# First quad's transposes in 64x64 tiles, and narrower idle matmuls around its first scores

## The chip, the cores and the metric

The kernel runs on one core of one Trainium2 chip. A core has five engines that run side by side: TensorE (PE in the profile, with its weight loads as PEld), VectorE (DVE), ScalarE (ACT), GpSimd (POOL) and SyncE (SP, which here only issues transfers). Sixteen DMA engines carry data between HBM and the core's memory, SBUF. TensorE writes its results to PSUM, which has eight banks, numbered 0 to 7. The metric is the device time of one execution, in microseconds (us); the median of several is compared.

## What is computed

A sigmoid attention over 8 batches of 12 heads (448 tokens, 64 numbers a head) is followed by a token mixer whose mixing matrix is made from its own input. All inputs and outputs are float32.

```python
def _attn_ref(q, k, v):
    S = q.shape[2]
    scale = 1.0 / np.sqrt(q.shape[-1])
    scores = scale * np.matmul(q, k.transpose(0, 1, 3, 2)) - np.log(S)
    attn = 1.0 / (1.0 + np.exp(-scores))
    return np.matmul(attn, v).astype(np.float32)

def _moe_ref(x, w_q, w_k, w_out):
    wq = x @ w_q
    wk = x @ w_k
    scale = 1.0 / np.sqrt(d_hyper)
    W_tok = scale * np.einsum('bsd,btd->bst', wq, wk)
    mixed = np.einsum('bst,btd->bsd', W_tok, x)
    return (np.maximum(mixed, 0.0) @ w_out).astype(np.float32)
```

The attention's output, with its heads side by side, is `x` of the second part.

## The kernel before

The work is cut into 24 quads, each with four heads of one batch (`quads`, numbered n). For a quad, q, k and v come in as float32 tiles of 448 KB (192 KB and 256 KB for the two pieces of the first quad's k), are cast to bfloat16 and, for q and k, transposed, so that the 64 numbers of a head lie along the partitions. A quad has seven score steps and seven value steps. One score step (`scores`) is four matmuls in 64x64 tiles of the array, 448 columns each, into a pair of PSUM banks, and one sigmoid on ScalarE over the pair (128x896), which writes bfloat16. One value step (`values`) is four such matmuls that add the sigmoid's output times v into a further pair of banks. The mixer's steps of the batches are threaded in between.

All engines' instructions are issued in the order in which the code stands; a hand-written string, `PLAN`, sets it, one letter per step. `S` is a score step, `P` or `p` a value step, `q` and `k` the transposes of a later quad's q and k by TensorE, `r` and `z` transposes by VectorE, `1` a cast on VectorE, `a` and `b` the transposes of the second quad's q and k. `F` is a matmul of zeros by zeros, 128x512, into a bank of its own (`spare`): nothing reads it. Which PSUM banks a step takes is listed in the same order in `BANKS`.

The loads are issued by SyncE in the order of the string `ORDER`, eight tiles in flight at most; a further load waits until the cast that reads its buffer's last tile has run. POOL does most of the casts (L192, L209, L215), from quad 2 on.

The start stands ahead of the plan. TensorE runs 32 matmuls of zeros (L690) while the first loads are under way. Then come the first quad's pieces: q is cast in two parts, tokens `IA` (four of seven blocks) on VectorE and `IB` (three) on ScalarE; k in two, `KA` (three) on VectorE and, later, `KB` (four), also on VectorE. `tr_part` transposes a part on TensorE and copies it out of PSUM into `qk[0]` (L804): `transposes_whole` uses the whole 128x128 array for each block of tokens, so that the two head halves of a block come out next to each other; `transposes`, which later quads use (line 229), takes four 64x64 tiles per block, and writes the two halves into two banks. `q` parts `IA` and `IB` and `k` part `KA` go before the plan's first letter; part `KB` is the letter `K`. The plan begins `FFSSSFFKSSF1S1ab`. A score step needs all of `qk[0]`'s q, and the block of k that it multiplies with: its first three need `KA` alone.

Of the kernel before, what the change touches and what calls it, by code (L numbers as in the profile page):

```python
# [17 lines left out]
def kernel(  # L18
# [12 lines left out]
    nc = tc.nc  # L31
# [4 lines left out]
    P = 128  # L36
    NI, NP = 7, 64
# [4 lines left out]
    HALF = (slice(0, 64), slice(64, 128))  # L42
# [21 lines left out]
    banks = ps_q.tile([P, 8, 512], F32, tag="banks", name="banks")  # L64
# [19 lines left out]
    def take(*ids):  # L84
        for b in ids:
            readers[b] = (readers[b][0] + readers[b][1], [])

    def bank2():
        lo, hi = (int(b) for b in BANKS.pop())
        take(lo, hi)  # L90
        assert hi == lo + 1
        return (lo, hi), banks[:, lo : hi + 1], banks16[:, lo : hi + 1]

    def bank1():
        b = int(BANKS.pop())
        take(b)
        return (b,), banks[:, b], banks16[:, b]

    def read(fb, inst, keep=False):

        for b in fb:
            for old in readers[b][0]:
                if not keep and old.ins.engine != inst.ins.engine:
                    tc.declare_no_dep(inst.ins, old.ins, reason="both only read the bank")
            readers[b][1].append(inst)
# [6 lines left out]
    zeros = singles.tile([P, 512], BF16)  # L112
# [12 lines left out]
    def xt(u, j):  # L125
# [4 lines left out]


    PLAN = (
        "FFSSSFFKSSF1S1abSSSSSPrPsPSPSzPqSkSSP1PSPSxPSrPSSPSPsPPPPPPP"
        "SPPSSzWWWSWWWSxSSrXSNPsPPPPSPSPUSzSPPPSRMSPPPSqkSSXMSSMSRPPC"
        "SP1xSPPPcSSWWWxSWdWSWSQSrNsSSOOOSPPPSPPSPzPISISISISPPPPPSPSc"
        "PodoSSxUSPPMSPRPSPPScWQWSdMSWWoWWSMPPSPPrPSPPSNQosSSzSQOQxSO"
# [84 lines left out]
    qk = {}  # L221
    ps_qk = {}

    def transposes(ps, t16, r):

        for x, i in enumerate(range(r.start, r.stop)):
            for g in range(2):
                for h in range(2):
                    nc.tensor.transpose(
                        ps[HALF[g], h, x * NP : (x + 1) * NP], t16[HALF[h], i, g, :],  # L230
                        ident16[HALF[h], HALF[h]],
                    )

    def transposes_whole(ps, t16, r):

        for x, i in enumerate(range(r.start, r.stop)):
            nc.tensor.transpose(
                ps[:, x * P : (x + 1) * P], t16[:, i].rearrange("p b d -> p (b d)"), ident16,
            )
# [75 lines left out]
    def scores(n, i):  # L315
        fb, sc, _ = bank2()
        for g in range(2):
            for h in range(2):
                nc.tensor.matmul(  # L319
                    sc[HALF[h], g, 0:S], qk[n][HALF[g], h, 1, i, :],  # L320
                    qk[n][HALF[g], h, 0].rearrange("p i n -> p (i n)"), start=True, stop=True,
                )
        at = at_bufs[len(sigmoids) % len(at_bufs)]
        inst = nc.scalar.activation(at, sc[:, :, 0:S], ACTF.Sigmoid, bias=attn_bias, scale=attn_scale)  # L324
        read(fb, inst)
        if len(sigmoids) >= len(at_bufs):

            tc.declare_no_dep(inst.ins, sigmoids[-len(at_bufs)].ins, reason="TensorE read the buffer in between")
        sigmoids.append(inst)
        ats[n, i] = at  # L330
# [3 lines left out]
    def values(n, i, tail, eng):  # L334
        u, j = quads[n]
        if i == 0:
            pv[n] = bank2()
        fb, ps, _ = pv[n]
        for h in range(2):
            for g in range(2):  # L340
                nc.tensor.matmul(  # L341
                    ps[HALF[g], h, 0:S], ld["v16", n][HALF[h], g, i, :],
                    ats[n, i][HALF[h], g, :], start=(i == 0), stop=(i == NI - 1),
                )
        if i == NI - 1:
            if tail:
                for h in range(2):
                    read(fb, COPY["vs"[h]](out=xt(u, j)[:, h, 0:S], in_=ps[:, h, 0:S]))
            else:
                read(fb, COPY[eng](out=xt(u, j)[:, :, 0:S], in_=ps[:, :, 0:S]))  # L350
# [323 lines left out]
    def cols(r):  # L674
# [9 lines left out]
        out=ident, in_=ident, compare_op=ALU.not_equal, fill=1.0, base=0,  # L684
# [1 line left out]
    )  # L686
    nc.vector.tensor_copy(out=ident16, in_=ident)
    nc.scalar.activation(warm, zeros[:, 0:1], ACTF.Sigmoid, bias=attn_bias, scale=1.0)
    for _ in range(32):
        nc.tensor.matmul(banks[:, 6, 0:P], zeros[:, 0:P], zeros[:, 0:P], start=True, stop=True)  # L690
    for t in xts:
        nc.vector.memset(t[:, :, S:], 0.0)
    for t in wqks:
# [76 lines left out]
    def pump():  # L770
        while pumped[0] < len(ORDER):
            nm, n = ORDER[pumped[0]]
            if (nm, n) not in OTHERS:
                if not ready(nm, n):
                    break
                cast_now(nm, n, "d" if (nm, n) in CASTING else "g")
            pumped[0] += 1

    def cast_next(e):
        nm, n = BY[e].pop(0)  # L780
        assert ready(nm, n) and (e == "v" or nm in "vw" or KIND[n] in "qa")
        cast_now(nm, n, e)
        pump()
# [16 lines left out]

    def tr_part(nm, t16, r, e):
        fb, _, ps = bank2()
        transposes_whole(ps[:, 0], t16, r)
        read(fb, COPY[e](  # L804
            out=qk[0][:, :, "qk".index(nm), r].rearrange("p h i n -> p i h n"),
            in_=ps[:, 0, 0 : (r.stop - r.start) * P].rearrange("p (i h n) -> p i h n", h=2, n=NP),
        ))

    tr_part("q", q016, IA, "v")
    tr_part("q", q016, IB, "s")  # L810
    tr_part("k", k016, KA, "v")
    cast_part(k016, k0, KB, "v")
    used |= {("q", 0), ("k", 0)}
# [6 lines left out]
    for t in PLAN:  # L820
        if t == "F":
            nc.tensor.matmul(bank1()[1], zeros[:, 0:P], zeros, start=True, stop=True)
            continue
        if t in "12":
            cast_next("vs"[int(t) - 1])
            continue
        kind = ALIKE.get(t, t if t in "qkx" else t.upper())
        c = done[kind]
        done[kind] += 1
        tail = done["S"] == N * NI  # L830
        if t == "S":
            scores(*divmod(c, NI))
        elif kind == "P":
            n, i = divmod(c, NI)
            values(n, i, tail or t == "R", "s" if t == "p" else "v")
            if i == NI - 1:
                used.add(("v", n))
                pump()
        elif kind in "qk":
            if t in "rs":  # L840
                quads_r.append(c) if t == "r" else None
                if t == "s":
                    quadrants(c, 0)
            tr(c, kind, t)
            if t in "df":
                used.add(("q", c))
            if t not in "cers":
                used.add((kind, c))
                pump()
        elif t == "g":  # L850
            move()
        elif t == "z":
            n = quads_r.pop(0)
            quadrants(n, 1)
            used.update({("q", n), ("k", n)})
            pump()
        elif t == "K":
            tr_part("k", k016, KB, "v")
        elif kind == "x":
            tr_x(c, tail, t in "XY", "s" if t in "yY" else "v")  # L860
        elif kind == "W":
            mlp_wqk(*divmod(c, NC), tail, t in "wl", t in "Ll")
        elif kind == "C":
            if c % 3 < 2:
                y, w = c % 3, slice(c // 3 * 3, c // 3 * 3 + 3)
                nc.sync.dma_start(out=wout16[HALF[y], w, 1], in_=wout16[HALF[1 - y], w, 0])
        elif kind == "N":
            mlp_wkn(c)
        elif kind == "U":
            (mlp_tmp_tiled if t in "Tt" else mlp_tmp)(c, t in "ut")  # L870
        elif kind == "M":
            u, x = divmod(c, NC // 2)
            mlp_mix(u, x, t == "m", tail or t == "G")
            if x == NC // 2 - 1:
                if u // 2 in TW:
                    chunks.extend((u // 2, ((u % 2, i), (u % 2, 6 - i))) for i in range(3))
                    if u % 2:
                        chunks.append((u // 2, ((0, 3), (1, 3))))
                else:
                    chunks.extend((u // 2, m, -1) for m in (range(3, NI) if u % 2 else range(3)))  # L880
        elif kind == "O":
            if (opened or chunks)[0][0] in TW:
                out_pair(t == "o", t == "Q")
            elif t in "Ii":
                out_halves(t == "i")
            else:
                out_chunk(t in "oQ", tail)
            if not opened:
                allowed[0] = 2
                pump_loads()  # L890
                pump()
# [29 lines left out]
```

## Time and profile before

| | |
|---|---|
| median of 3 runs | 182.27 us (181.79 to 182.78) |
| the profiled execution's own time | 182.08 us |
| its span, first to last instruction | 180.3 us |
| TensorE matmuls busy | 168.8 us, 3431 of them |
| ScalarE busy | 161.0 us |
| VectorE busy | 144.7 us |
| GpSimd busy | 117.4 us |
| bytes moved by DMA | 47.31 MB, mean 262 GB/s |

The profile shows one execution. A row of its timeline gives the start (us from the span's start), the busy time, the engine, the source line, the operation, output and input tiles, the count of instructions, and in brackets the idle time before it with what ended it. Rows of PE overlap, since matmuls are pipelined. The chain of waits follows the work that ended last back from the end: each piece is what the next one had been waiting for, or what ran just before it on the same engine. A row of the stretches' view gives the start and end, the length, the busy time of each engine with its count of instructions, the granted clock of TensorE, and the busy share of the DMA engines.

### The profile page before, as it was taken

Reading aid. Unit: us, or ns where it says so; the run is one execution under the profiler, and the core shown is the slowest. Engines: PE = TensorE matmul, PEld = TensorE weight load, DVE = VectorE, ACT = ScalarE, POOL = GpSimd, SP = SyncE. Lnnn points to the kernel's source line nnn. Section 1 sums busy time; section 2 is a strip of 40 time slices with the busy share of each in tenths; the row PEclk is TensorE's granted clock in tenths of the full one; section 3 lists DMA queues with packets and bytes.
Section 4 is the critical chain, followed back from the end, with each engine's and each line's share of the span. In section 5 each row is a group of like instructions: output and inputs, shape, how many; then the busy total and the mean of one; then the engine's idle time right before and its main releaser. Section 6 shows DMA issues by size and latency. Waiting matters only on the chain.

```text
span 180.3 us, 7877 instructions
## 1 busy us (share of the span) xinstructions
PE 168.8 (94%) x3431; PEld 116.1 (64%) x3431; DVE 144.7 (80%) x230; ACT 161.0 (89%) x213; POOL 117.4 (65%) x160
## 2 busy tenths in 40 slices
PE   7867799989999999999999999999999999999990
PEld 7433456454476465656667788788888878787560
DVE  3667899999998899989989799987897976678401
ACT  4699999999999999999999999999999999966250
POOL 1074798992899999999999999999879410010000
PEclk9999999999999999999999999999999999999999
DMA  5999999998998899999999929779997432405686
GB/s 168 345 396 385 329 382 397 398 233 181 349 386 296 312 284 346 305 319 275 266 407 323 335 81 276 284 209 315 278 333 204 114 91 62 120 4 126 165 242 175
DMA packets 24787, 47.31 MB, mean 262 GB/s; under 512 B 3760, under 2 KB 18352, under 8 KB 24752
## 3 DMA queue, kind: packets, MB, share of 16 engines
q1 hardware_dynamic: 23472, 44.64, 76.3%
q0 software_dynamic: 800, 1.18, 3.6%
q10 hardware_dynamic: 480, 0.98, 1.7%
q8 instruction: 27, 0.44, 1.0%
q14 instruction: 8, 0.07, 0.1%
HBM read 35.78 MB, written 11.01 MB: 260 GB/s over the span
## 4 chain that ended last, share of the span: by engine, by line
PE 78%; DVE 13%; ACT 5%; issue 1%
PE banks L319 16%; PE banks L530 15%; PE banks L341 13%; PE banks L612 13%; ACT at L324 5%; PE banks L571 3%; PE banks L416 3%; DVE xt L350 3%; DVE qk L245 3%; PE banks L363 2%; PE banks L379 2%; PE banks L690 2%; PE banks L404 2%; PE banks L460 2%; DVE mx L471 2%; PE banks L484 1%
## 5 line engine op out<-in xcount | busy, mean ns | idle before, releaser
L324 ACT ACTIVATE at<-banks 128x896 bf16<-128x896 f32 x168 | 140.3, 940 | 2.0 <-PE banks L319 1.3
L319 PE MATMUL banks<-qk 64*64 64x448 bf16 x672 | 62.5, 357 | 5.1 <-ACT at L324 2.5
L341 PE MATMUL banks<-at,v 64*64 64x448 bf16 x672 | 45.7, 350 | 0.4 <-ACT at L324 0.4
L319 PEld LDWEIGHTS <-qk 64*64 64x64 bf16 x672 | 26.4, 105 | 24.2 <-issue 14.9
L530 PE MATMUL banks<-wout,mx 64*64 64x384 bf16 x672 | 36.1, 323 | 0.0
L192 POOL CAST qk<-k 128x896 bf16<-128x896 f32 x19 | 22.8, 1202 | 10.1 <-DMA k<-in_k_dram 9.7
L341 PEld LDWEIGHTS <-v 64*64 64x64 bf16 x672 | 23.7, 106 | 6.9 <-POOL v L209 0.8
L530 PEld LDWEIGHTS <-mx 64*64 64x64 bf16 x672 | 23.9, 107 | 3.5 <-issue 0.5
L192 POOL CAST qk<-q 128x896 bf16<-128x896 f32 x18 | 21.6, 1197 | 4.4 <-DVE qk L276 4.0
L350 DVE CAST xt<-banks 128x896 bf16<-128x896 f32 x21 | 22.6, 1081 | 2.2 <-PE banks L341 2.0
L612 PE MATMUL banks<-wout,mx 128*128 128x384 bf16 (+1 forms) x138 | 24.1, 320 | 0.0
L471 DVE TENSOR_SCALAR mx<-banks 128x1024 bf16<-128x1024 f32 (+3 forms) x23 | 21.2, 933 | 2.9 <-PE banks L484 1.9
L209 POOL CAST v<-v 128x896 bf16<-128x896 f32 x21 | 19.4, 933 | 1.6 <-DMA v<-in_v_dram 1.3
L612 PEld LDWEIGHTS <-mx 128*128 128x128 bf16 x138 | 12.5, 98 | 9.6 <-issue 2.5
L245 DVE STREAM_TRANSPOSE qk<-qk 32x448 f32<-32x448 f32 x28 | 17.8, 636 | 0.8
L161 POOL COPY swap<-qk 32x448 uint32<-32x448 uint32 x26 | 14.7, 565 | 2.8 <-DVE qk L192 1.3
L276 DVE STREAM_TRANSPOSE qk<-qk 128x448 f32<-128x448 f32 x26 | 16.1, 629 | 0.1
L164 POOL COPY qk<-qk 32x448 uint32<-32x448 uint32 x26 | 14.4, 554 | 1.5
L167 POOL COPY qk<-swap 32x448 uint32<-32x448 uint32 x26 | 14.4, 552 | 1.5
L413 POOL COPY wq<-wqk 64x448 bf16<-64x448 bf16 x3 | 1.7, 554 | 17.7 <-DVE wqk L412 17.7
L645 ACT COPY o<-banks 128x384 f32<-128x384 f32 x13 | 6.3, 483 | 5.7 <-PE banks L612 4.9
L392 DVE COPY xn<-banks 128x1024 bf16<-128x1024 bf16 (+1 forms) x15 | 9.5, 632 | 1.6 <-PE banks L379 1.4
(88 smaller groups left out, 203.3 us busy)
## 6 DMA issues: line engine op xcount, KB each, us to landing
q<-in_q_dram SPq DMA_DIRECT2D x24, 448.0 KB, 6.8
v<-in_v_dram SPq DMA_DIRECT2D x24, 448.0 KB, 6.7
k<-in_k_dram SPq DMA_DIRECT2D x23, 448.0 KB, 6.3
out_dram<-o SPq DMA_DIRECT2D x50, 192.0 KB, 4.1
wout<-in_moe_w_out_dram POOLq DMA_DIRECT2D x2, 576.0 KB, 9.1
wout<-wout SPq DMA_DIRECT2D x4, 288.0 KB, 9.8
out_dram<-o ACTq DMA_DIRECT2D x4, 192.0 KB, 3.5
k<-in_k_dram SPq DMA_DIRECT2D x1, 256.0 KB, 4.5
```

Of the source, the lines that this page charges most:

```text
L161: eng.tensor_copy(out=z[lo], in_=w[hi, 0])
L192: COPY[e](out=f[:, :, "qk".index(nm)].rearrange("p e i d y -> p e y i d"), in_=ld.pop((nm, n)).rearrange("p (y i e d) -> p e y i d", y=2, ...
L209: COPY[e](out=t16.rearrange("p b i d -> p (b i d)"), in_=ld.pop((nm, n)).rearrange("p b x -> p (b x)"),)
L245: nc.vector.transpose(out=qk[n][other : other + 32, h].rearrange("p t i n -> p (t i n)").bitcast(F32), in_=w[own : own + 32, 1 - h],)
L276: nc.vector.transpose(out=qk[n][:, t].rearrange("p t i n -> p (t i n)").bitcast(F32), in_=w)
L319: nc.tensor.matmul(sc[HALF[h], g, 0:S], qk[n][HALF[g], h, 1, i, :], qk[n][HALF[g], h, 0].rearrange("p i n -> p (i n)"), start=True, stop=True,
L324: inst = nc.scalar.activation(at, sc[:, :, 0:S], ACTF.Sigmoid, bias=attn_bias, scale=attn_scale)
L341: nc.tensor.matmul(ps[HALF[g], h, 0:S], ld["v16", n][HALF[h], g, i, :], ats[n, i][HALF[h], g, :], start=(i == 0), stop=(i == NI - 1),)
L350: read(fb, COPY[eng](out=xt(u, j)[:, :, 0:S], in_=ps[:, :, 0:S]))
L471: inst = nc.vector.tensor_scalar(dst, ps, moe_scale, 0.0, ALU.mult, ALU.max)
L530: nc.tensor.matmul(ps[HALF[x], y, 0:NB], mx[HALF[y], u, b, 64 * (i - 3 * y) : 64 * (i - 3 * y) + 64], wout16[HALF[y], b // 2, swapped(y, b ...
L612: nc.tensor.matmul(ps, mxs[w][:, 2 * S * c + m * P : 2 * S * c + (m + 1) * P], wout16[:, c, 0, w0:w1], start=(c == 0), stop=(c == NC - 1),)
```

## The change

Four things are changed; the order of the steps, the banks and the loads stay as they are.

- The first 32 matmuls of zeros (128 columns each, 4096 in all) become eight of 128 columns and six of 512 (4096 in all).
- `tr_part` uses `transposes` in place of `transposes_whole`: four 64x64 transposes for each block of tokens in place of one 128x128, 56 in place of 14 for the first quad.
- The copies in `tr_part` read two PSUM banks, with the tokens of one head half in one piece, in place of one bank with the two halves side by side. The number of elements stays.
- The plan's first four `F` become `f`: each is two matmuls of 64x64 tiles with 256 columns, one for each half of the output partitions, in place of one 128x128 matmul with 512. The fifth `F`, after the fifth score step, stays.

```diff
@@ PLAN @@
-        "FFSSSFFKSSF1S1abSSSSSPrPsPSPSzPqSkSSP1PSPSxPSrPSSPSPsPPPPPPP"
+        "ffSSSffKSSF1S1abSSSSSPrPsPSPSzPqSkSSP1PSPSxPSrPSSPSPsPPPPPPP"
@@ ahead of the loads @@
-    for _ in range(32):
-        nc.tensor.matmul(banks[:, 6, 0:P], zeros[:, 0:P], zeros[:, 0:P], start=True, stop=True)
+    for w in [P] * 8 + [4 * P] * 6:
+        nc.tensor.matmul(banks[:, 6, 0:w], zeros[:, 0:P], zeros[:, 0:w], start=True, stop=True)
@@ tr_part @@
         fb, _, ps = bank2()
-        transposes_whole(ps[:, 0], t16, r)
+        transposes(ps, t16, r)
         read(fb, COPY[e](
-            out=qk[0][:, :, "qk".index(nm), r].rearrange("p h i n -> p i h n"),
-            in_=ps[:, 0, 0 : (r.stop - r.start) * P].rearrange("p (i h n) -> p i h n", h=2, n=NP),
+            out=qk[0][:, :, "qk".index(nm), r].rearrange("p h i n -> p h (i n)"),
+            in_=ps[:, :, 0 : (r.stop - r.start) * NP],
         ))
@@ the plan's loop @@
         if t == "F":
             nc.tensor.matmul(bank1()[1], zeros[:, 0:P], zeros, start=True, stop=True)
+            continue
+        if t == "f":
+            spare = bank1()[1]
+            for y in HALF:
+                nc.tensor.matmul(spare[y, 0 : 2 * P], zeros[HALF[1], 0:NP], zeros[HALF[1], 0 : 2 * P], start=True, stop=True)
             continue
```

VectorE's instructions keep their places. This is a piece of its order, with the changed one marked + (a name's number tells tiles of one name apart and is different in the two programs; the last figures are the pattern that is written):

```order
-L789 CAST q_176<-q_123 128x2x4x64
-L789 CAST k_177<-k_124 128x2x3x64
-L804 COPY qk<-banks 128x4x2x64
-L804 COPY qk<-banks 128x3x2x64
-L789 CAST k_177<-k_124 128x2x4x64
+L789 CAST q_158<-q_123 128x2x4x64
+L789 CAST k_159<-k_124 128x2x3x64
+L804 COPY qk<-banks 128x2x256
+L804 COPY qk<-banks 128x2x192
+L789 CAST k_159<-k_124 128x2x4x64
```

The two copies write in runs of 256 and 192 elements where they wrote runs of 64; nothing has moved past anything. TensorE's program grows from 6864 to 6920 rows (a weight load and a matmul are a row each): the first matmuls lose 36 rows, the transposes gain 84 and the idle matmuls 8.

## The prediction

> **What bounds the kernel now.** I read the page first, then the chain of waits from the start, then the timeline of the stretch in which the chain leaves the changed code. The page says what kind of bound to expect:
>
> ```profile
> span 180.3 us, 7877 instructions
> PE 168.8 (94%) x3431; PEld 116.1 (64%) x3431; DVE 144.7 (80%) x230; ACT 161.0 (89%) x213; POOL 117.4 (65%) x160
> PE 78%; DVE 13%; ACT 5%; issue 1%
> ```
>
> TensorE carries 78% of the chain, but its 94% is an average. The chain in order of time shows three stages, of which these are the first rows:
>
> ```profile
> 4.61 1.25 PE banks L237 x10
> 5.86 0.47 PE banks L822 x2
> 6.33 0.39 PE banks L319 x4
> 6.74 9.83 ACT at L324 x12
> 16.62 0.38 PE banks L319 x4
> 17.00 0.28 PE banks L229 x28
> 17.31 1.09 DVE qk L307
> 18.43 1.08 DVE qk L192
> 19.51 0.98 DVE xt L350
> 20.53 0.48 PE banks L379 x32
> ```
>
> First the changed code (transposes L237, idle matmuls L822, the first score step L319), which ends when ScalarE begins its sigmoids at 6.74. Then ScalarE sets the pace. At 17.31 the chain passes to VectorE, with the copy of quad 3's transposed q and k (L307). What VectorE does from 22 to 40 us stands in one row, beside the loads' share:
>
> ```profile
> 4.10:9.00 4.90, 4.36 (x44) 2.44 (x42) 3.13 (x8) 3.25 (x5) 0.00 (x0) 1.00 0.99 334
> 9.00:16.80 7.80, 5.48 (x99) 2.89 (x102) 5.25 (x9) 7.80 (x11) 5.14 (x5) 1.00 1.04 393
> 22.00:40.00 18.00, 16.52 (x334) 9.57 (x330) 17.61 (x26) 17.80 (x23) 16.13 (x22) 1.00 1.06 358
> ```
>
> VectorE is busy 17.61 of 18.00 us, and the DMA engines are full (shares 0.99, 1.04, 1.06) from 4.1 us on. So a start that comes earlier is worth something only if it brings L307 at 17.31 forward, for behind it VectorE has no idle time in which to lose or regain anything much.
>
> **The change at its own place.** These are the rows of the start:
>
> ```profile
> 0.99 3.59 PE L690 MATMUL banks<-zeros 128*128 128x128 bf16 x32 [0.99 <-DVE zeros L680]
> 4.13 0.43 DVE L789 CAST q<-q 128x512 bf16<-128x512 f32 x1 [2.04 <-DMA q<-in_q_dram]
> 4.61 0.66 PEld L237 LDWEIGHTS <-q 128*128 128x128 bf16 x7 [0.29 <-DVE q L789]
> 4.64 0.36 DVE L789 CAST k<-k 128x384 bf16<-128x384 f32 x1
> 5.25 0.42 DVE L804 COPY qk<-banks 128x512 bf16<-128x512 bf16 x1 [0.25 <-PE banks L237]
> 5.57 0.48 ACT L804 COPY qk<-banks 128x384 bf16<-128x384 bf16 x1 [0.94 <-PE banks L237]
> 5.89 0.36 DVE L804 COPY qk<-banks 128x384 bf16<-128x384 bf16 x1 [0.21 <-PE banks L237]
> 6.30 0.33 PEld L319 LDWEIGHTS <-qk 64*64 64x64 bf16 x12 [0.50 <-DVE qk L804]
> 9.48 0.39 PEld L237 LDWEIGHTS <-q 128*128 128x128 bf16 x7 [0.20 <-DVE k L215]
> ```
>
> *Opening matmuls.* 32 x 128 and 8 x 128 + 6 x 512 are both 4096 columns, so I take the same end, 4.58. They are covered by q's load and cast, which end at 4.56. A coarser last matmul can move this by about 0.1 either way.
>
> *Transposes.* Ten wide ones take 1.25 us in the chain. The seven weight loads beside them take 0.66 at 4.61, but 0.39 at 9.48: TensorE still runs slow at the start, by 0.66 / 0.39 = 1.7, though the clock column reads 1.00. The nearest price for 64x64 tiles is quad 3's k, 28 transposes with 0.32 us of weight loads (row below), 11.4 ns each; slow, 19.4 ns. The 16 of q's first part are then out after 0.18 to 0.31 us and a tail of some 0.1 to 0.2 (0.42 of matmul less 0.32 of loads, at the slow rate twice that). So VectorE's copy of q begins at 4.9 to 5.1 by TensorE; by VectorE's own order not before 5.00, when its cast of k ends. I take 5.1 instead of 5.25. It ends at 5.5. The 12 transposes of k have come out by then (28 of q end by 5.15, then 0.23 and a tail), so k's copy runs from 5.5 to 5.9 in place of 5.89 to 6.25.
>
> *Copies.* They have as many elements as before. The same two-bank source is read by L307: 1.09 us for 1792 elements, 0.61 ns each; the wide form's 0.42 for 512 is 0.82 with its fixed part in it. I take 0.42 and 0.36 again, within 0.03 either way.
>
> *Idle matmuls.* The chain names the two `F` (0.47), but they only fill the wait: the first score's weights wait for VectorE's copy (0.50 before 6.30). Four 64x64 matmuls with 256 columns have half the columns of each `F` and run two beside each other; I give them nothing on the path, and up to 0.1 if they should run one after another.
>
> Summed, the first scores start at about 5.95 in place of 6.30, and ScalarE at 6.4 instead of 6.74: 0.35 us earlier, between 0.2 (VectorE's copies no quicker, TensorE slow) and 0.45 (5.00 + 0.42 + 0.36 + 0.05 = 5.83). For the later part of k (`K`) the same holds; it feeds the fourth score step, and ScalarE, once begun, runs 12 sigmoids without a stop (9.83 us, 0.82 each), so nothing waits for it.
>
> **What becomes of those 0.35 us.** Here the timeline decides:
>
> ```profile
> 12.27 0.93 POOL L209 CAST v<-v 128x896 bf16<-128x896 f32 x1
> 12.29 1.17 DVE L269 STREAM_TRANSPOSE qk<-qk 128x448 f32<-128x448 f32 x2 [1.04 <-POOL qk L192]
> 13.49 2.64 DVE L245 STREAM_TRANSPOSE qk<-qk 32x448 f32<-32x448 f32 x4
> 13.57 0.94 POOL L215 CAST q<-q 128x896 bf16<-128x896 f32 x1 [0.37 <-DMA q<-in_q_dram]
> 15.80 0.94 POOL L215 CAST k<-k 128x896 bf16<-128x896 f32 x1 [1.29 <-DMA k<-in_k_dram]
> ```
>
> and of the next microseconds:
>
> ```profile
> 16.62 0.38 PE L319 MATMUL banks<-qk 64*64 64x448 bf16 x4 [0.40 <-ACT at L324]
> 16.79 0.32 PEld L229 LDWEIGHTS <-k 64*64 64x64 bf16 x28
> 16.81 0.42 PE L229 MATMUL banks<-ident,k 64*64 64x64 bf16 x28
> 17.31 1.09 DVE L307 COPY qk<-banks 128x1792 bf16<-128x1792 bf16 x1 [1.18 <-PE banks L229]
> ```
>
> L307 waits for the transposes of quad 3's k, and their weight loads begin at 16.79. POOL's cast of that k ends at 15.80 + 0.94 = 16.74; 0.05 us later they run. The chain of waits leads back over the score step at 16.62, which ScalarE released, because it is what stood before them on TensorE; but had it come 0.35 earlier, the transposes would still have waited for POOL. POOL in turn sat idle for 1.29 us until the load landed, and that load's time is set by the full DMA engines, not by an engine in the changed code:
>
> ```profile
> 4.36 0.66 SPq L179 DMA_DIRECT2D v<-in_v_dram  x1
> 5.07 0.60 SPq L179 DMA_DIRECT2D q<-in_q_dram  x1
> 5.80 0.66 SPq L179 DMA_DIRECT2D k<-in_k_dram  x1
> ```
>
> ```profile
> DMA to landing us min/median/max: 7.8/8.3/9.9
> ```
>
> The second answer is on these three loads: least, median and most time from issue to landing. The last, quad 3's k, is the slowest, 5.80 + 9.9 = 15.7. SyncE issues it right behind the loads ahead of it, which the change leaves alone. So the 0.35 us shrink to the 0.02 between 16.79 and 16.81, and the rest becomes idle time: of TensorE ahead of those transposes, then of ScalarE at about 21 us, where its next scores stand behind L379, which waits for VectorE.
>
> **A side effect in the loads.** TensorE's program has 56 rows more by the fourth score step. It arrives in blocks, through the same DMA engines, and one of them shows in 13 to 15 us, none in 9 to 13:
>
> ```profile
> q1 hardware_dynamic: 330, 0.76, 101.5%
> q8 instruction: 1, 0.02, 3.5%
> ```
>
> 3.5% of 16 engines over 2 us is 1.12 us of one engine. The landings fit: from the first of the three loads (7.8 after 4.36) to the second (8.3 after 5.07, by POOL 13.5) are some 1.2 us, from the second to the last 2.2. So the late landing, on which everything hangs, holds about 1.0 us of waiting for one engine that fetched code. The page counts 27 such blocks for 6864 rows, one per 254. With 56 more rows this fetch is due some 56 rows earlier, 2 to 3 us. Then v of quad 0 and q of quad 3 may land 1.1 later too, and quad 2's q with them, while quad 3's k still lands at 15.7. What would follow: VectorE's L269 and L245 end at 13.49 + 2.64 + 1.1 = 17.23, ahead of 17.31 by 0.08; v's cast ends at 14.3 in place of 13.2, and the score steps behind its value steps are late by a few tenths that the 0.35 pay. So I cost this at nothing, between -0.45 (the fetch misses the k load and L307 comes as early as the start allows) and +0.3 (cover of 0.08 gone, by the width of a landing).
>
> **The sum.** The profiled execution took 182.08: its span of 180.3 and 1.8 around it. Less 0.02 it stays 182.1. The median of the runs is 0.19 above that execution, so 182.2 for the median. A difference below 0.5% (0.9 us) is about what a measurement of this kernel can tell from no change; the three runs alone reach from 181.79 to 182.78.
>
> **The rivals.**
>
> *Carried through* (chance 0.20). Nothing downstream takes the gain; L307 runs 0.35 earlier, 0.45 at most, and the time is 181.9. For it speaks the chain, which passes through ScalarE and not POOL; against it the 1.29 us that POOL waited. It needs k's load to land 0.3 earlier. Even then it is 0.2%, less than can be told.
>
> *A slow clock* (0.13), on the other side. The `F` keep TensorE busy while it waits for copies; the change takes most of that away and shortens the transposes. If TensorE stays slow beyond the first scores, rows price it: at 1.7 times, the 5.48 us that it is busy from 9.0 to 16.8 become 9.3 in 7.8, 1.5 too many, less the lead of 0.35: 1.2 us, 183.4. Up to 9.0 it costs nothing, since ScalarE needs one score step each 0.82 us and a slow one takes 0.7 (1.7 x 0.39). It decides, that is, passes 0.9 us, if the clock stays low to about 15 us. Against it: with the low clock TensorE would have hardly a gap, so the cause would remove itself.
> The Trainium skill, "TensorE: Matmul & The Clock Gate", Part 1, says that the clock is released only after a window of about 3.4 us of sustained activity. Row 4.61 against row 9.48 agrees that TensorE starts out slower; how much idling it forgives no row here shows. By that rule alone, with the window missed once, the low clock would end near 9 us and cost nothing; missed twice, it is the 183.4 above.
>
> *Later loads* (0.08). The earlier fetch of code hits a load for which the cover is less than 1.1 us, for instance by landing twice in the loads ahead of 15.7, and VectorE's L245 end late: 0.3 to 1.1 us, 182.5 to 183.3.
>
> *It doesn't do what it says* (0.04). The transposes are bound by VectorE's order, the scores start at 6.3 as before: 182.2.
>
> **How the numbers follow.** My forecast, absorbed at the k load, has 0.50, with a range of its own of 181.7 to 182.8, as wide as the runs. Something not seen that makes it faster gets 0.05. Within 0.5%: 0.47 of the forecast, 0.15 of the carried gain, 0.04 of no effect, 0.02 of later loads: 0.68. Slower: 0.13, 0.06 and 0.02 of the forecast's spread: 0.21. Faster: 0.05, 0.05 of the carried gain with a quick run, 0.01: 0.11. The range for 8 in 10 reaches from the carried gain with the runs' spread, 181.4, to the slow clock, 183.4.
>
> **What would show it.** Right: the first sigmoid at 6.3 to 6.5; POOL's cast of quad 3's k still at 15.8; L229's weight loads for k at 16.8, L307 at 17.3, and the gap of ScalarE near 21 us longer by about 0.3. Wrong: L307 before 17.1 (carried, or the fetch elsewhere) or after 17.6 (loads); seven weight loads of L237 near 9 us that take 0.66 and not 0.39 (clock); copies L804 of over 0.5.

## The result, and the profile after

| | before | after |
|---|---|---|
| median of 22 runs each, side by side | 182.20 us (181.58 to 184.89) | 183.49 us (182.50 to 185.72) |
| ratio, 95% interval | | 1.0068 (1.0040 to 1.0095) |
| the profiled execution's own time | 182.08 us | 185.36 us |

The kernel became slower by 0.7%. The profiled execution of after is one of its longest, 1.9 us above the median, so what follows shows each of the losses, but not how much of each an average execution has. Each run also gives the mean granted clock of TensorE over the execution; where the text says "whole clock" it means 0.994 or more, and a lower mean says that some stretch ran at half speed (0.987 in this execution).

These lines of the page of after stand against those shown of before:

```profile
span 183.6 us, 7932 instructions
PE 169.4 (92%) x3458; PEld 114.4 (62%) x3459; DVE 144.7 (79%) x230; ACT 161.1 (88%) x213; POOL 117.4 (64%) x160
PEclk9979999999999999999999999999999999999998
...
q8 instruction: 27, 0.44, 1.1%
...
PE 68%; ACT 21%; DMA 4%; DVE 3%; issue 2%; ACTq 0%; SPq 0%; DVEq 0%
```

The engines' work is the same (VectorE 144.7 in both, ScalarE 161.1 for 161.0), while the span is 3.3 us longer: what came is waiting. The chain has a new carrier, DMA with 4%, where before named none, and the clock row has a 7 in its third slice.

**The start.** The timeline of after from 4.5 to 18 us:

```profile
4.51 0.44 PEld L229 LDWEIGHTS <-q 64*64 64x64 bf16 x28 [0.83 <-DVE q L789]
5.20 0.84 DVE L804 COPY qk<-banks 128x512 bf16<-128x512 bf16 x2
6.09 0.33 PEld L319 LDWEIGHTS <-qk 64*64 64x64 bf16 x12 [0.52 <-DVE qk L804]
6.53 4.96 ACT L324 ACTIVATE at<-banks 128x896 bf16<-128x896 f32 x6 [0.92 <-PE banks L319]
8.31 0.59 PE L319 MATMUL banks<-qk 64*64 64x448 bf16 x4 [0.19 <-ACT at L324]
12.02 6.58 ACT L324 ACTIVATE at<-banks 128x896 bf16<-128x896 f32 x8 [0.53 <-PE banks L319]
13.36 0.93 POOL L209 CAST v<-v 128x896 bf16<-128x896 f32 x1 [1.12 <-DMA v<-in_v_dram]
14.72 0.94 POOL L215 CAST q<-q 128x896 bf16<-128x896 f32 x1 [0.43 <-DMA q<-in_q_dram]
15.87 0.93 POOL L215 CAST k<-k 128x896 bf16<-128x896 f32 x1 [0.22 <-PE banks L319]
17.73 1.09 DVE L307 COPY qk<-banks 128x1792 bf16<-128x1792 bf16 x1 [1.61 <-PE banks L229]
```

The first sigmoid begins at 6.53 (before 6.74). ScalarE, which ran 12 sigmoids without a stop before, now stops for 0.53 ahead of 12.02, and L307 is 0.42 late (17.73 for 17.31). The score step at 8.31 shows the reason: 0.59 for four matmuls that take 0.38 at full speed. The stretches say when TensorE ran at half speed (columns: start and end, length, busy time of each engine with its count, clock, DMA share, GB/s), first of after:

```profile
4.90:8.30 3.40, 2.16 (x68) 1.19 (x61) 2.44 (x6) 2.25 (x4) 0.00 (x0) 1.00 1.00 366
8.30:11.70 3.40, 2.92 (x26) 1.92 (x26) 1.35 (x3) 3.20 (x4) 1.81 (x2) 0.50 1.04 400
11.70:16.00 4.30, 3.00 (x48) 1.32 (x45) 4.13 (x7) 3.98 (x5) 2.54 (x4) 1.00 1.05 387
```

and of before:

```profile
2.40:5.80 3.40, 3.37 (x32) 3.11 (x30) 1.21 (x3) 0.74 (x2) 0.00 (x0) 1.00 0.97 301
5.80:9.20 3.40, 2.88 (x34) 1.06 (x32) 2.12 (x5) 2.71 (x5) 0.00 (x0) 1.00 1.02 381
9.20:12.60 3.40, 2.43 (x39) 1.37 (x38) 1.65 (x4) 3.40 (x6) 2.67 (x3) 1.00 1.04 395
```

From 8.3 to 11.7 the clock of after is 0.50; in the 3.4 us ahead of it TensorE was busy 2.16 us, 64%. In before the stretches stay at 85% and 71%, and the clock at 1.00. The busy share alone doesn't decide it, though: from 11.72 to 15.13 TensorE of after is busy for 2.12 of 3.41 us, 62%, and the clock stays up. In this execution the half-speed stretch made ScalarE stop, and with it after lost what it had won, and 0.42 more, at 17.7; but this was regained: by 45 us the same instruction of VectorE runs 0.02 earlier than in before. The 3.3 us of this execution were lost later.

**At 92 us.** TensorE's timeline of after:

```profile
91.03 0.36 PE L319 MATMUL banks<-qk 64*64 64x448 bf16 x4
92.84 0.76 PE L341 MATMUL banks<-at,v 64*64 64x448 bf16 x12 [1.45 <-issue]
```

TensorE stands still for 1.45 us and waits for nothing that the profile knows ("issue"); no such row stands in before. The view of transfers from 88 to 93 us has this of the queues:

```profile
q1 hardware_dynamic: 503, 1.34, 102.8%
q8 instruction: 1, 0.02, 1.8%
```

The code queue (q8) moved one block of TensorE's program, 1.8% of 16 engines over 5 us, or 1.4 us of one engine, and the engines were full (102.8%). From the records of that queue and the row numbers of the program I worked out that every block is 256 rows, and that the block is due when TensorE passes row 256n - 68 (only the last block of some programs began up to 1.7 us sooner than that). Without it TensorE ran to row 256n + 192, 260 rows further, and stopped. In after this block (n = 11) was due at 83.53 and came between 89.91 and 91.39. TensorE had used up its rows with row 3008 = 256 x 11 + 192 at 91.03, and went on 1.45 us after the block had landed. In before the same block was due at 84.58, began at 88.09 and had landed at 89.38, 3.2 us before TensorE came to the next row, at 92.5.

**At 175 us.** The chain of after has this step, and beneath it stand the waits of ScalarE's output copies from 165 to 180 us in after:

```profile
171.03 4.17 DMA out_dram<-o
```

```profile
ACT o L645 <- PE banks L612: 4.6, 4, 2.8
ACT o L645 <- DMA out_dram<-o: 2.1, 1, 2.1
```

and in before (columns: total us, times, longest):

```profile
ACT o L645 <- PE banks L612: 4.9, 6, 2.9
ACT o L645 <- DMA out_dram<-o: 0.8, 1, 0.8
```

A copy (L645) writes one of three `o` buffers and waits until the store that read it last has landed. That wait grew from 0.8 to 2.1 us, and the copy ahead of the last matmuls is late by it. (What waits is told by the row; how much of it reaches the end is worked out below.) Here too a code block moved: in after from 169 to 174 us, in before only from 172 to 177.

```profile
q8 instruction: 1, 0.02, 1.8%
```

```profile
q8 instruction: 1, 0.02, 1.2%
```

The first row is of after, the second of before. The last block, for the 6844th row, came at 171.44 in after, among the stores on which the copy waits; in before at 175.34, behind them.

### The profile page after: what moved, and what is told of

Same layout as the page of the kernel before. It is cut to its first block, busy times and chain, and to the rows that moved or that the text cites. A ratio compares the mean times of both kernels' runs of the same rounds, so it can differ in the third digit from the quotient of the medians.

```text
span 183.6 us, 7932 instructions
## 1 busy us (share of the span) xinstructions
PE 169.4 (92%) x3458; PEld 114.4 (62%) x3459; DVE 144.7 (79%) x230; ACT 161.1 (88%) x213; POOL 117.4 (64%) x160
## 4 chain that ended last, share of the span: by engine, by line
PE 68%; ACT 21%; DMA 4%; DVE 3%; issue 2%; ACTq 0%; SPq 0%; DVEq 0%
ACT at L324 20%; PE banks L319 16%; PE banks L530 15%; PE banks L341 13%; PE banks L612 8%; DMA out_dram<-o 2%; PE banks L416 2%; PE banks L571 2%; DMA k<-in_k_dram 2%; PE banks L363 2%; PE banks L404 2%; PE banks L379 2%; PE banks L460 2%; PE banks L484 1%; DVE mx L471 1%
## 5 line engine op out<-in xcount | busy, mean ns | idle before, releaser
L319 PE MATMUL banks<-qk 64*64 64x448 bf16 x672 | 63.7, 360 | 5.1 <-ACT at L324 2.1
L645 ACT COPY o<-banks 128x384 f32<-128x384 f32 x13 | 6.1, 483 | 6.7 <-PE banks L612 4.6
```

The source lines that it names most:

```text
L319: nc.tensor.matmul(sc[HALF[h], g, 0:S], qk[n][HALF[g], h, 1, i, :], qk[n][HALF[g], h, 0].rearrange("p i n -> p (i n)"), start=True, stop=True,
```

## The experiments

Two theories stood against each other. The first: the 56 rows more of TensorE's program move every code block against the loads and stores; that costs the waits at 92 and 175 us, whatever else changed (a form of it says that the block at 83 to 92 us is late because of the copies of `wout` within SBUF, 288 KB each). The second: the emptier start makes the clock fall, and the time is lost there. A third is the rival of the prediction that a gain at the start is carried through. The pieces of code show the lines that tell what was changed; `...` stands for further lines. All kernels ran 6 or 12 times, beside 29 to 35 runs of before.

**56 rows more, and nothing else.** Before, with 60 small idle matmuls at the start in place of 32.

```diff
-    for _ in range(32):
-        nc.tensor.matmul(banks[:, 6, 0:P], zeros[:, 0:P], zeros[:, 0:P], ...)
+    for m, w in [(P, P)] * 4 + [(64, 64)] * 56:
+        nc.tensor.matmul(banks[0:m, 6, 0:w], zeros[:, 0:m], zeros[:, 0:w], ...)
```

> The kernel before, with its opening 32 matmuls of zeros cut into 60 (4 of 128 columns, 56 of 64; 4096 columns as before), so that TensorE's program has 56 rows more, as in the changed kernel, and nothing else differs. Theory 1 (where the blocks of TensorE's code end): the time follows the count of rows, so this kernel is slower than before by as much as the changed one, 0.4 to 1.0% (183.0 to 184.0), and code blocks arrive where they did in the changed kernel, the first between 10 and 11.5 us instead of 13.3. Theory 2 (TensorE's clock falls back because it idles between the shorter steps): no difference from before, within 0.3%.

Measured: 183.35 us, ratio 1.0014 (0.9983 to 1.0046). By the ratio alone this is no difference, for the before beside it had a lower clock in 10 of its 29 runs. Of the runs with whole clock, the median is 182.85 (9 runs) against 182.12 (19). The first code block came at 12.22, not at the 10 to 11.5 that was expected. In the profiled execution the first sigmoid is 0.47 late (7.21): the two `F` ahead of it took 1.06 us, in place of 0.68 in before. By 45 us this is regained. The stop at 92 us is missing, and the chain passes through a store late in the program:

```profile
168.93 3.59 DMA out_dram<-o
```

**After, with 200 rows more**, which is 256, one whole block, more than before, so that the blocks lie against the work as in before.

```diff
-    for w in [P] * 8 + [4 * P] * 6:
+    for m, w in [(32, 36)] * 114:
...
```

> The changed kernel, with its opening 14 matmuls cut into 114 of 36 columns (4104 columns in all), so that all that follows stands 256 rows, one whole block of code, behind its place in the kernel before. Theory 1 (where the blocks end): as fast as before, within 0.3% (181.7 to 182.7), with code blocks at 13 to 14 and at 88 us as in the profile before. Theory 2 (clock): slower than before by 0.4 to 1.0%, with score steps of 0.59 us between 8 and 12 us.

Measured: 182.66 us, ratio 1.0001 (0.9964 to 1.0037). All four parts of the change are in it, and the loss is gone from the ratio, whose interval lies below that of after (1.0040 to 1.0095). Of its 8 runs with whole clock one took 184.01 us, longer than any such run of before, so a long run is rarer here but not gone. In its profile neither the stall at 92 us nor the wait at 171 us is seen, though its clock was at half speed from 14.5 to 17.9 us.

**After, with the wide idle matmuls again** (same 6920 rows).

```diff
-        "ffSSSffKSSF1S1ab...
+        "FFSSSFFKSSF1S1ab...
...
-    for w in [P] * 8 + [4 * P] * 6:
+    for m, w in [(P, P)] * 8 + [(P, P)] + [(P, 96)] * 4 + [(P, 4 * P)] * 5:
...
```

> The changed kernel, with the four wide idle matmuls F put back for f, and eight rows of opening matmuls added, so that the count of rows is the changed kernel's. Theory 1 (where the blocks end): as slow as the changed kernel, 0.4 to 1.0% over before. Theory 2 (clock): the clock stays up between 8 and 12 us, score steps there take 0.38 us, and the time is that of before within 0.3%.

Measured: 183.37 us, ratio 1.0029 (0.9990 to 1.0068), which falls between what the two theories had expected. The runs with whole clock have a median of 182.78 (7 runs). The profiled execution kept its clock (busy 2.75 us of 3.4 where after had 2.16), and begins better than before: L307 at 16.90, 0.41 earlier. The tail took it back:

```profile
ACT o L645 <- DMA out_dram<-o: 2.9, 2, 2.2
```

So the loss of the tail does not need the clock to fall. The row is that of the waits from 165 to 180 us.

**128 rows more on before**, half a block.

```diff
-    for _ in range(32):
+    for m, w in [(32, 43)] * 96:
...
```

> The kernel before, with its opening 32 matmuls cut into 96 of 43 columns (4128 columns), so that TensorE's program has 128 rows more, half a block of code. Theory 1 (where the blocks end): the time differs from before by more than 0.3%, to which side can't be told ahead. Theory 2 (clock): no difference from before, within 0.3%.

Measured: 185.39 us, ratio 1.0141 (1.0096 to 1.0186): twice the loss of the change, from idle matmuls at the start. Its clock was at full speed throughout in the profiled execution (4 of the 6 runs had a lower one). TensorE's timeline shows the stall of after, at another line, since it is not the work that decides it but the row:

```profile
88.56 0.26 PE L431 MATMUL banks<-ident,wqk 64*64 64x64 bf16 x6
90.16 0.22 PE L431 MATMUL banks<-ident,wqk 64*64 64x64 bf16 x2 [1.34 <-issue]
```

The block was due at 81.90 and came between 87.32 and 88.64. TensorE stopped after row 3008 again, though another line stands there, and went on 1.52 us after the landing; in the third such stop, of after with four `o` buffers (0.52 us, at 92.66), it was row 3008 and 1.48 us. This kernel stopped twice more, after row 4800 and after row 5056, both again 256n + 192, until 130.59 and 136.79, each 1.5 us after a block had landed. (The profile lists 0.53 us without a matmul for the first, which it puts down to ScalarE, and 0.33 for the second.)

**The coarser opening matmuls alone.**

```diff
-    for _ in range(32):
+    for w in [P] * 8 + [4 * P] * 6:
...
```

> The kernel before with one part of the change alone, the opening matmuls (8 of 128 columns and 6 of 512). TensorE's program is 36 rows shorter than before, so each block of code arrives later and the last boundary (row 6844) lies beyond the program's 6828 rows. Theory 1 (where the blocks end): no block of code arrives during the last output stores; time as before or up to 0.4% less (181.5 to 182.6). Theory 2 (clock): no difference from before, within 0.3%.

Measured: 182.09 us, ratio 0.9990 (0.9965 to 1.0016), and none of the 12 runs had a lower clock. This part costs nothing. In the profiled execution L307 begins 0.29 earlier than in before, and 0.11 of it is still there at 165 us. Its first sigmoid is at 6.45 with the wide transposes, earlier than after's 6.53. It has 26 blocks, the last at 165.0, so none among or behind the stores, and still waits 0.8 us for one there, as before does: so that much of the wait isn't a block's doing. Both theories had expected this time.

**After and before without three of the four copies of `wout`.** The place that they fill is zeroed instead, so the mixer's result is another; the diff is that of both kernels.

```diff
+    nc.gpsimd.memset(wout16[:, :, 1], 0.0)
...
-            if c % 3 < 2:
+            if c % 3 < 2 and c < 1:
```

> The changed kernel, with three of the four copies of the output weights inside SBUF (at 79 to 83 us) left out and their place set to zero on GpSimd at the start, so its output is not the reference's. Theory 1a (the block of code that TensorE needs near 91 us is late because it queues behind those copies): no stall of TensorE there, the runs above 184 are gone and the median falls by 0.3 us or more against the changed kernel; what is left over before, 0.3 to 0.8 us, comes from the last block. Theory 1b (it is late for another reason, such as the loads): the median stays at 183.2 to 183.7, with runs above 184.5.

> Control for the run above: the kernel before with the same three copies left out (output not the reference's). Both theories: 0 to 0.6 us less than before, 181.6 to 182.6; the difference of the two kernels without copies tells how much of the change's cost does not go through the copies.

Measured: 184.67 us, ratio 1.0144 (1.0110 to 1.0177), from after; 183.59 us, ratio 1.0074 (1.0045 to 1.0103), from before. Both are slower, not faster as was expected, because the zeroing stands in the way: in the kernel made from before the first sigmoid is 1.70 late. The pair differs by 1.08 us, hardly less than after and before themselves (1.29). The profiled execution of the kernel made from after has no stall near 92 us, but one execution cannot tell that, since the stall comes and goes (below). Nothing here shows that these copies make the block late; as the start was disturbed, it isn't excluded either.

**After, and before, with four `o` buffers.**

```diff
-    p_o = pool("o", 3)
+    p_o = pool("o", 4)
```

> The changed kernel with four buffers for the output tiles in place of three. Theory 1c (the last block of code, 4 us earlier than before, delays an output store, and ScalarE's copies near 172 us wait for that store's buffer): the wait of 0.7 to 2.2 us before ScalarE's copies at L645 is gone, and the time falls by 0.4 to 1.0 us against the changed kernel, to 182.4 to 183.0. Otherwise: no change from the changed kernel, 183.2 to 183.7.

> Control for e8 and e10: the kernel before with four buffers for output tiles. Both theories: no difference from before, within 0.2%, as its last block of code comes at 175 us, behind the stores that would be waited for (0.8 us are waited for a store in before's profile, of which up to 0.3 may be won).

Measured: 183.55 us, ratio 1.0060 (1.0026 to 1.0093), of after with four; 182.18 us, ratio 0.9999 (0.9980 to 1.0019), of before with four. The wait of the tail is gone from the profile of the first, but the time is not the 182.4 to 183.0 that theory 1c expected; it lies where no change was expected. 8 of its 12 runs had a lower clock, and the profiled one lost two stretches, from 7.65 to 14.48 us. That gives the price of a slow clock that lasts that long, in one execution: 1.24 us at L307, 0.81 to 0.86 left from 45 us on. For before, the fourth buffer does nothing: where the last code block comes behind the stores, nothing waits for a buffer long enough to matter.

**The narrow idle matmuls alone.** Before with `f` for its first four `F`.

```diff
-        "FFSSSFFKSSF1S1ab...
+        "ffSSSffKSSF1S1ab...
...
```

> The kernel before with one part of the change alone: the four narrow idle matmuls f in place of F (8 rows more, so the blocks of code end nearly where they did). If the narrow ones let TensorE's clock fall back: a window of half clock in half of the executions or more (granted clock 0.991 or lower; before has it in about a quarter), and a median 0.3 to 0.6 us over before. If only the rows count: time and clock as before, within 0.3%.

Measured: 182.28 us, ratio 0.9999 (0.9969 to 1.0029); one of the 12 runs took 217.73 us at a clock of 0.758 over the whole execution, which no other kernel here showed. 4 of 12 had a lower clock, before beside it 5 of 35. So the narrow ones alone neither cost time nor lose the clock in half of the executions. The profiled execution differs from before by 0.02 at L307.

**The wide idle matmuls and four `o` buffers on after**, that is, the kernel with wide idle matmuls of above and a fourth buffer.

> The kernel of e3 (the change with F in place of f, 6920 rows) with four buffers for output tiles in place of three. If the last block of code costs by way of an output store whose buffer ScalarE waits for: no wait over 0.3 us for a store before ScalarE's copies at L645, and 0.4 to 0.8 us less than e3 took over before, so 0 to 0.2% over before. If the tail is not where the rows cost: 0.4% over before, as e3.

Measured: 183.12 us, ratio 1.0057 (1.0022 to 1.0091), with a lower clock in 7 of 12. That is not the 0 to 0.2% over before that was expected if the tail is where the rows cost. With whole clock alone the median is 182.36 (5 runs) against 182.78 with three buffers (7 runs), and 182.62 (4) against 182.94 (11) for after: in the expected direction both times, but too few runs to tell. So what the fourth buffer wins is not shown in the times. The profiled execution has the whole clock, 182.18 us and no wait on a store; the copy that waited 2.1 us in after shows this in ScalarE's timeline:

```profile
171.40 0.48 ACT L645 COPY o<-banks 128x384 f32<-128x384 f32 x1 [0.65 <-PE banks L612]
```

**64x64 transposes only for the two parts on VectorE ahead of the plan**, with 6870 rows, six more than before, and the wide idle matmuls kept.

```diff
-        transposes_whole(ps[:, 0], t16, r)
+        if e == "s" or r == KB:
+            transposes_whole(ps[:, 0], t16, r)
+            ...
+            return
+        transposes(ps, t16, r)
```

> The kernel before with the change's opening matmuls (36 rows fewer) and the 64x64 transposes for the first part of q and the first part of k alone (42 rows more), F kept: 6870 rows, so the blocks of code end where they did, within 6 rows. If rows and clock are what made the change slow: no slower than before, 181.7 to 182.3, with the first sigmoid at 6.4 to 6.6. If the 64x64 transposes themselves cost: slower than before by 0.3% or more.

Measured: 182.52 us, ratio 1.0005 (0.9976 to 1.0034), with the first sigmoid at 6.28; 3 of 12 had a lower clock, the profiled one among them (0.77 late from 45 us on). With almost the rows of before, there is no stall like that at 92 us. But it does wait on stores at the tail, and so does the kernel with the narrow idle matmuls alone; the row of each, in this order:

```profile
ACT o L645 <- DMA out_dram<-o: 2.1, 2, 1.4
```

```profile
ACT o L645 <- DMA out_dram<-o: 1.7, 2, 0.9
```

In both, the last block began sooner than in before, too, at 174.23 and 172.63 in place of 175.34. In the profiled executions with three `o` buffers the wait goes with that block: where it begins at 175.34 or later, or doesn't exist, ScalarE waits 0.8 us for stores; where it begins between 169.5 and 174.3 it waits 1.7 to 3.8 us, except with 56 rows more (0.7). But the wait isn't the loss: the end is later for it by 0.2 us and nothing in these two, and by 0.2 with 128 rows more, which waits longest.

**What they say together.** This table compares the start of the same instruction with that in before (us, + is later), in one profiled execution each:

| at (us, before) | after | +56 rows | after +200 | wide idle | +128 rows | after, four `o` | wide idle, four `o` |
|---|---|---|---|---|---|---|---|
| 17.3 | +0.42 | +0.47 | +1.13 | -0.41 | +0.25 | +1.24 | +0.31 |
| 45.0 | -0.02 | -0.04 | +0.45 | -0.18 | -0.19 | +0.81 | -0.13 |
| 88.3 | +0.11 | +0.08 | +0.57 | -0.17 | -0.06 | +0.86 | 0.00 |
| 97.8 | +1.75 | +0.09 | +0.57 | -0.17 | +1.47 | +1.58 | 0.00 |
| 137.7 | +2.42 | +0.32 | +0.64 | +0.22 | +2.87 | +1.66 | +0.03 |
| 165.2 | +2.42 | +0.33 | +0.80 | +0.23 | +2.88 | +2.12 | +0.03 |
| end of the span | +3.3 | +0.6 | +0.9 | +1.1 | +3.1 | +2.2 | +0.1 |

With 128 rows more, the 1.4 us between 97.8 and 137.7 are lost where its two further stops are. A shorter one of the same kind stands in after (row 4800, 0.22 us without a matmul, ahead of 132.48), where 0.5 of its 0.67 are lost, and with wide idle matmuls (row 4032, 0.19 us ahead of 115.95), where 0.35 of its 0.39 are. In before no block brings TensorE to a stop.

The stall at 92 us comes and goes between executions of programs with the same rows: of the five here with 6920 it is there in after and after with four `o`, and not in the three others. From 165 us to the end the three of them with three `o` buffers lose 0.3 to 0.9, the two with four at most 0.1; the program whose blocks lie as in before (+200) loses 0.1.

The runs with whole clock show the same without a trace. Of before's 72, from the three sessions, none is above 183.41 us. Of these five programs with 6920 rows, 11 of 36 are above 183.5: after itself has seven from 182.50 to 183.07 and four from 183.88 to 185.13. The four programs with 6828 to 6872 rows have none of 40 there, the one with 7120 one of 8. So most executions of after lose some 0.3 to 0.9, about what the tail costs, and some 1.7 to 3.0; that the second kind are those with a stall like the one at 92 us fits its size, but no trace of such a run with the whole clock was taken.

The second theory is likely to hold beside the first. A lower clock is found in 35 of 70 runs of the five programs whose first transposes are all in 64x64 tiles (after, with 200 rows more, with wide idle matmuls, and with four buffers both ways), and in 29 of 141 of before and those with the wide transposes (56 rows more, opening alone, narrow idle alone, four buffers; the kernels with 128 rows more and with zeroing are left out, since their stalls and late start disturb the clock themselves). So it goes with the transposes more than with the idle matmuls: with the wide `F` back it is still 12 of 24. But how often the clock falls differs between the sessions: in the first, 9 of 24 runs with 64x64 transposes stand beside 10 of 29 of before, no difference, in the other two 15 of 24 beside 11 of 64. So the second theory is borne out by counts, not shown by a run that changes the clock and nothing else.

An estimate of the shares, from the medians of the runs: with whole clock after takes 182.94 and before 182.1, 0.8 more; with a lower clock some 0.9 more than with a whole one in either (183.78 for after, 182.87 to 183.79 for before), in 50% of the runs in place of 23%, which makes 0.9 x 0.27 = 0.24. So the code blocks may have about three quarters of the loss and the clock one quarter; this is rough, for the two sum to 1.04 of the 1.29, and the first takes all that the runs with whole clock lose for the blocks' doing.

What stays open is which of the tail's late stores are the code's doing, why the block near 90 us begins some 2 to over 6 us after it is due from execution to execution, and which transfer holds its engine.

## Why the prediction failed

It gave 182.2 with 181.4 to 183.4, and no measurable change as the likeliest; the time is 183.49 and 0.7% slower. By its steps:

*The opening matmuls* end where they did (0.99 + 3.60 against 0.99 + 3.59), and alone give 0.9990: right.

*The transposes and copies*, first sigmoid at 6.3 to 6.5: it is 6.53 in after and 6.32 with the wide idle matmuls, where the copies of q and k take 0.75 together. The gain was 0.21 in place of 0.35, at the lower end of its range. In after k's cast waited 0.53 for its load, until 4.93. And the coarser opening with the wide transposes began its sigmoids at 6.45, so that the gain comes from the transposes isn't shown.

*The idle matmuls* of the new form cost nothing on the path, as predicted (alone 0.9999). The reason, that the wide ones only fill a wait, is not always so: with 56 rows more the two `F` took 1.06 us, and the first scores started only at 6.68, 0.38 after the last copy of q and k had ended.

*What becomes of the 0.35*: that quad 3's k load takes it agrees with after by number, where the load landed at 15.7 and POOL's cast began at 15.87 (predicted 15.8), but this was luck. That cast no longer waited for its load (POOL was at q's cast until 15.66), and L307 was late by a score step at 17.04, behind ScalarE's stop. Nor does it hold in others: with wide idle matmuls that cast came at 15.44, L307 at 16.90, and 0.17 us were still ahead at 98 us. The rival "carried through" is that case, with 0.2 in place of its 0.35, and a stop at 115.95 and the tail used it up.

*A side effect in the loads*, "So I cost this at nothing", is the step that failed. Its first half came out to the figure: the first block moved from 13.3 to 10.35 us, v of quad 0 and q of quad 3 were cast 1.1 later (13.36 for 12.27, 14.72 for 13.57) and k of quad 3 as before. But I moved one block out of 27, the first, and asked what it delays; the others move by the same 56 rows. Two of them were where it hurts: the one near 90 us, which in before landed 3.2 us ahead of the row that needs it, with 1.5 us of that gone by the restart, and the last, which went among the stores. The page of before had the count of blocks, and the wait of 0.8 on a store at the tail was to be seen. Priced by the table, they are 0.3 to 0.9 at the tail (how much of that is the block's doing stays open), and between 88 and 98 us 0.7 and 1.6 in the two executions that stalled. The term was put at nothing, between -0.45 and +0.3; with whole clock, after took 0.8 us more than before.

*A slow clock*, 0.13: the clock does fall, in 11 of 22 executions of after and in 21 of 93 of before; its time and price were otherwise. It isn't that TensorE stays slow from the start: the clock was up and fell again at 8.3, 7.65 or 14.5 us. The price for two lost stretches, 1.2 us, was 1.24 at L307 but 0.81 to 0.86 downstream. With one, after had regained all of it by 45 us, but the kernels with 200 rows more and with two parts in 64x64 tiles, which lost it at 14 to 18 us, kept 0.45 and 0.77. "Up to 9.0 it costs nothing" looked only at ScalarE's need. The Trainium skill, "TensorE: Matmul & The Clock Gate", Part 1, gives one idle window of about 3.4 us as what brings the half rate back: the length agrees (8.31 to 11.72 here), while "idle" was a stretch in which TensorE was busy for 2.16 of 3.40 us, and one with 2.12 of 3.41 us, from 11.72, did not bring it back.

*Later loads*, 0.08, was the nearest to the cause, and was priced for the start alone.

The Trainium skill, "Runtime: NRT & Kernel Launch", "Instruction fetch mechanics", has the blocks of 256 instructions on an own queue; the 27 packets with 0.44 MB agree. It calls their fetch mostly hidden; here the stalls of 1.45 and 1.34 us are not.

## What to carry to other kernels

An edit that adds rows to one engine's program early on moves every later block of its code against the transfers: look not only at the first one, but at each place where the DMA engines are full, or where a buffer waits for a store. To tell such a loss from the edit's own work, add the same number of rows, or rows up to a whole block, as idle instructions at the start. And before a stretch of idle work is cut, look at TensorE's busy share in each 3.4 us: in the profiled executions here, up to 165 us, the clock fell after all three stretches with 49 to 51%, and after two of the 22 with 57 to 66%, so a low share is a risk, but no share was found that decides it.

## What the runs showed that I had not expected

- TensorE can run out of program: 1.45 us and 1.34 us without a matmul, released by "issue", when a block began 6.4 and 5.4 us after it was due. Being late is common: in before the blocks began 0.3 to 4.2 us late, and none made TensorE stop. It stopped where a block landed less than some 1.5 us before its rows were used up: it went on 1.2 to 1.5 us after the landing.
- 128 rows of idle work at the start cost 1.4% (185.39 us), 256 rows more than before none that can be told (1.0001, with the whole change in it).
- The clock of after fell after 3.4 us in which TensorE was busy 64%, and held after the next such stretch, with 62%. In the five profiled executions with a fall it stayed low for 3.41 or 6.83 us.
